# Down projection of a fused attention and feed-forward kernel: tokens as the stationary operand, or weights as the stationary operand with tokens streamed

## The chip, the core and the metric

The kernel runs on one core of one Trainium2 chip. The metric is the device time of one execution in microseconds. TensorE (PE) multiplies and can only write PSUM; VectorE (DVE) and ScalarE (ACT) work on SBUF and PSUM; GpSimd (POOL) does little here; SyncE (SP) issues nearly all DMAs from one queue, in order. A matmul has a stationary operand, loaded into the array by a weight load (PEld in the profile), and a streamed operand whose columns pass through; it may use a part of the array's rows or columns.

## What is computed

x has 2048 tokens of 576 features. The output is x plus two branches of the same layer-normalised x. All is bfloat16.

```python
xn = _layernorm(x, axis=-1)
return x + _A_ref(xn, A_wqkv, A_wo) + _B_ref(xn, B_w_gate, B_w_up, B_w_down)

def _B_ref(x, w_gate, w_up, w_down):          # F = 4608
    g = _silu(x @ w_gate)
    u = x @ w_up
    return (g * u) @ w_down
```

Branch A is attention in 32 heads of 18 features, in which each token looks at itself and at seven earlier ones, two apart (`W, dil = 8, 2`), followed by a product with `wo` (576 x 576).

## The kernel before, in words

Token 16p + r lies in partition p, row r (`R = 16`), so that a 128-token tile is one row of all partitions. The 16 rows are worked in four quarters of 4 rows, 512 tokens (`NTT = 4`, `TT = 512`).

First comes a stage for all tokens: layer norm, transposes into `xnT` (features in partitions), and the q, k, v products (`p_row`, L310). Then for each quarter `tt` of the loop at the end:

- **gate/up**: nine chunks (`NCH`) of four 128-feature tiles. `g_pair` (L611) makes gate and up for two tiles at a time, with the weights `gu` stationary and the quarter's 512 tokens of `xnT` streamed. `g_evac` takes them out of PSUM: ACT applies SiLU (L622) and copies up (L623), DVE multiplies (L624) into `hT`, which holds 36 tiles of 128 features by 512 tokens.
- **down**: for each row `sub`, `d_half` (L640) makes 128 tokens by 576 features: the 128 tokens of `hT` are stationary and 288 columns of `wd` are streamed, over 36 tiles, and then the same over five tiles of the attention output `oT` (which takes the place of `xnT`) with `wo`. The fifth tile of `oT` has its 64 features twice, in the lower and the upper 64 partitions, so that either half of the array's rows can use them.

All large matmuls are halves: one uses 64 rows of the array, its partner the other 64, each into its own bank. With `swap` 0 lower rows make the first bank and upper rows the second; with `swap` 1 they change over, so after both passes every bank holds the sum over all rows. A bank must not be written by both halves at once, so a GpSimd no-op waits for the first pass and the second pass waits for it (`fence_after`, `fence_before`). The second pass leaves the fifth `oT` tile out, since the first has covered both banks with it.

PSUM has eight banks, given out in turn (`new_ps`). A gate/up pair takes four, two rows of the down stage take four. `d_out` adds the residual rows `xr` on DVE (L652) into `ot`, and SP stores one row (L655); in the last row TensorE adds the residual by an identity product and ACT and DVE copy out (L654).

The attention itself is DVE work: `chain(tt)` puts it as a list of closures into `dve` (`Filler`), and `dve.pump(us)` in the loops above emits as much of it as the credit allows, so its place in DVE's queue is fixed when the program is written out: 1.4 us after each `g_evac`, 12.5 and 4.0 us ahead of the two `d_out` of a pair of rows. The chain of quarter tt + 1 is added after chunk 1 of quarter tt. It goes: eight products of `QO` with rows of `Kr` (L418), each with two sums (L423); a mask (L430), maximum, difference, exponential on ACT, sum, reciprocal, product (L438 to L446); eight products with `Vr` (L450) and seven sums (L455), the last of which writes the output over q in `QOP`. `done` doubles the last 64 features into the padding of `QOP`.

At the last chunk of a quarter SP transposes that quarter's four rows of `QOP` into `oT` (L669), loads `xr` in two pieces (L671), and loads the weights of a later chunk: `load_gu(it + 2)` (L182 to L185) comes after each chunk and waits until the chunk's two-deep slot of `gu` is free. In the down stage the stores (L655) stand on SP behind DVE's adds, with a ring load (L398) of the attention between them.

Of the kernel before, what the change touches and what calls it, by code (L numbers as in the profile page):

```python
# [9 lines left out]
bf16 = mybir.dt.bfloat16  # L10
f32 = mybir.dt.float32
ACT = mybir.ActivationFunctionType
ALU = mybir.AluOpType
# [4 lines left out]
P = 128  # L18
H, DH, W, DIL = 32, 18, 8, 2
D = H * DH  # L20
# [4 lines left out]
KT = 5  # L25
DPAD = KT * P
# [4 lines left out]
RT = 4  # L31
NTT = R // RT
TT = RT * P
# [37 lines left out]
def kernel(  # L71
# [11 lines left out]
    nc = tc.nc  # L83
# [3 lines left out]
    NF = F // P  # L87
    NCH = NF // FC

    x_v = A_x.rearrange("b (p r) d -> p (b r) d", r=R)  # L90
    out_v = out.rearrange("b (p r) d -> p (b r) d", r=R)

    const = ctx.enter_context(tc.tile_pool(name="const", bufs=1))
    big = ctx.enter_context(tc.tile_pool(name="big", bufs=1))
# [11 lines left out]
    QOP = big.tile([P, R, DPAD], bf16, name="QO")  # L106
# [3 lines left out]
    hT = big.tile([P, NF, TT], bf16, name="hT")  # L110
    wd = big.tile([P, NF, D], bf16, name="wd")
    wo = big.tile([P, KT, D], bf16, name="wo")
# [2 lines left out]
    mx = big.tile([P, RT, H], f32, name="mx")  # L115
    ssum = big.tile([P, RT, H], f32, name="ssum")
    gu = big.tile([P, NSLOT, 9, FC * P], bf16, name="gu")
    xr = big.tile([P, RT, D], bf16, name="xr")
    kv_d = dram.tile([2, NTT - 1, P, RT * D], bf16, name="kv_d")


# [1 line left out]
    XC, XN = RT * D, RT * DPAD  # L123
# [9 lines left out]
    stage = [hTf[:, o + i * XC:o + (i + 1) * XC].rearrange("p (r d) -> p r d", d=D) for i in range(4)]  # L133
    L = PP[:, 1, 0:2 * W * RT * H].bitcast(f32).rearrange("p (w r h) -> p w r h", w=W, r=RT)
    oT = xnT
    xcT = PP[:, 0, 0:DPAD].rearrange("p (k t) -> p k t", t=P)
    xn0 = A[:].rearrange("p w r h -> p (w r h)")[:, 0:DPAD]

# [40 lines left out]
    def load_gu(it):  # L179
        ch, slot = it % NCH, it % NSLOT  # L180
        fc = slice(ch * FC * P, (ch + 1) * FC * P)
        nc.sync.dma_start(gu[:, slot, 0:4, :], B_w_gate[0:512, fc].rearrange("(kt kp) n -> kp kt n", kp=P))  # L182
        nc.sync.dma_start(gu[:, slot, 4:8, :], B_w_up[0:512, fc].rearrange("(kt kp) n -> kp kt n", kp=P))
        nc.sync.dma_start(gu[0:64, slot, 8, :], B_w_gate[512:576, fc])
        nc.sync.dma_start(gu[64:128, slot, 8, :], B_w_up[512:576, fc])  # L185
# [10 lines left out]
    def new_ps(name):  # L196
        return ps.tile([P, 512], f32, name=name, tag="ps")
# [124 lines left out]
    def fence_after(mm):  # L322
        f = nc.gpsimd.engine_nop()
        tc.add_manual_dep(f.ins, mm.ins.name, SYNC, reason="first half done")
        return f

    def fence_before(mm, f):
        tc.add_manual_dep(mm.ins, f.ins.name, SYNC, reason="banks change row tiles")
# [66 lines left out]
    def ring_load(m, tt):  # L395
        ring = Kr if m == 1 else Vr
        s0 = (HALO + RT * tt) % NRING
        nc.sync.dma_start(ring[:, s0:s0 + RT, :], kv_d[m - 1, tt - 1].rearrange("p (r d) -> p r d", d=D))  # L398


    dve = Filler()
    chains = [0]

    def pieces(tt, w):
        s = (HALO + RT * tt - 2 * w) % NRING
        n = min(RT, NRING - s)
        return [(0, n, s)] + ([(n, RT, 0)] if n < RT else [])

    def chain(tt):
        rows = slice(RT * tt, RT * tt + RT)  # L410
        prod = PP[:, 0, :].rearrange("p (r c) -> p r c", c=D)
        acc = PP[:, 1, :].rearrange("p (r d h) -> p r d h", d=DH, h=H)
        pv = PP[:, 0, :].rearrange("p (r d h) -> p r d h", d=DH, h=H)
        Lr = L.rearrange("p w r h -> p r h w")

        def mul(w):
            for a, b, s in pieces(tt, w):
                nc.vector.tensor_tensor(prod[:, a:b], QO[:, RT * tt + a:RT * tt + b, :],  # L418
                                        Kr[:, s:s + b - a, :], op=ALU.mult)

        def red(w, h):
            rs = slice(2 * h, 2 * h + 2)
            nc.vector.tensor_reduce(L[:, w, rs], prod[:, rs].rearrange("p r (h d) -> p r h d", d=DH),  # L423
                                    axis=AX.X, op=ALU.add)

        def mask():
            for w in range(1, W):
                n = min(RT, max(0, 2 * w - RT * tt))
                if n:
                    nc.vector.memset(L[0:1, w, 0:n, :], NEG)  # L430

        bc = lambda t: t[:].unsqueeze(1).to_broadcast([P, W, RT, H])
        for w in [0] + list(range(W - 1, 0, -1)):
            dve.add(1.3, lambda w=w: mul(w))
            for h in range(2):
                dve.add(1.2, lambda w=w, h=h: red(w, h))
        dve.add(0.4, mask)
        dve.add(1.2, lambda: nc.vector.tensor_reduce(mx[:], Lr, axis=AX.X, op=ALU.max))  # L438
        dve.add(1.2, lambda: nc.vector.tensor_tensor(L, L, bc(mx), op=ALU.subtract))  # L439
        if tt + 1 < NTT:  # L440
            dve.add(0.0, lambda: ring_load(1, tt + 1))
        dve.add(2.0, None)
        dve.add(1.0, lambda: nc.scalar.activation(L, L, ACT.Exp, scale=SCALE))  # L443
        dve.add(1.2, lambda: nc.vector.tensor_reduce(ssum[:], Lr, axis=AX.X, op=ALU.add))
        dve.add(0.3, lambda: nc.vector.reciprocal(ssum[:], ssum[:]))
        dve.add(1.2, lambda: nc.vector.tensor_tensor(A[:], L, bc(ssum), op=ALU.mult))  # L446

        def pvm(w, dst):
            for a, b, s in pieces(tt, w):
                nc.vector.tensor_tensor(dst[:, a:b], Vr[:, s:s + b - a, :].rearrange("p r (d h) -> p r d h", h=H),  # L450
                                        A[:, w, a:b].unsqueeze(2).to_broadcast([P, b - a, DH, H]), op=ALU.mult)

        def pva(w):
            dst = acc if w else QO[:, rows, :].rearrange("p r (d h) -> p r d h", h=H)
            nc.vector.tensor_tensor(dst, acc, pv, op=ALU.add)  # L455

        for w in range(W - 1, -1, -1):
            dve.add(1.4, lambda w=w: pvm(w, acc if w == W - 1 else pv))
            if w < W - 1:
                dve.add(1.3, lambda w=w: pva(w))  # L460
        if tt + 1 < NTT:
            dve.add(0.0, lambda: ring_load(2, tt + 1))

        def done():
            nc.vector.tensor_copy(QOP[:, rows, D:DPAD], QOP[:, rows, 512:D])
            chains[0] += 1
        dve.add(0.3, done)
# [15 lines left out]
    def turn(r):  # L483
        return lambda: transp_halves(r)
# [20 lines left out]
    t = [new_ps("qkv_ps") for g in range(NG)]  # L505
# [39 lines left out]
    t = p_row(2, turn(3))  # L545
# [6 lines left out]
    t = p_row(3, turn(4))  # L552
# [10 lines left out]
    for r in range(4, R):  # L563
        t = p_row(r)
# [53 lines left out]
    def g_evac(ch, j):  # L618
        t = ring_ps[j]
        sg = tmp.tile([P, TT], bf16, name="sg", tag="sg", bufs=3)  # L620
        uc = tmp.tile([P, TT], bf16, name="uc", tag="uc", bufs=3)
        nc.scalar.activation(sg[:], t[0][:], ACT.Silu)  # L622
        nc.scalar.copy(uc[:], t[1][:])  # L623
        nc.vector.tensor_tensor(hT[:, ch * FC + j, :], sg[:], uc[:], op=ALU.mult)  # L624
# [22 lines left out]
    def d_out(r, sub, t):  # L647
# [6 lines left out]
            (nc.scalar.copy, nc.vector.tensor_copy)[h](ot[:, cols], t[h][:, 0:HALF])  # L654
        nc.sync.dma_start(out_v[:, r, :], ot[:])  # L655

    for tt in range(NTT):
        for ch in range(NCH):
            it = tt * NCH + ch
            for p in range(2):  # L660
                g_pair(tt, ch, p)
                for j in (2 * p, 2 * p + 1):
                    g_evac(ch, j)
                    if it % NCH < NCH - 1 or p == 0:
                        dve.pump(1.4)
            if ch == NCH - 1:
                dve.drain(lambda: chains[0] > tt)
                for r in range(RT * tt, RT * tt + RT):
                    nc.sync.dma_start_transpose(oT[:, :, r * P:(r + 1) * P], QOP[:, r, :])  # L669
                for i in (0, 2):  # L670
                    nc.sync.dma_start(xr[:, i:i + 2, :], x_v[:, RT * tt + i:RT * tt + i + 2, :])  # L671
            if it + NSLOT < NTT * NCH:
                load_gu(it + NSLOT)
            if tt == 0:
                if 1 <= ch <= 7:
                    load_wd(ch - 1)
                if ch in (3, 4):
                    load_wd(11 - ch)
                for _ in range(3 if ch in (1, 2) else 2):
                    if wo_order:  # L680
                        load_wo(wo_order.pop(0))
                if ch == 0:
                    store(2, 3, 3)
            if ch == 1 and tt < NTT - 1:
                chain(tt + 1)
        for sub in range(0, RT, 2):
            t, fence = {}, {}
            for swap in range(2):
                for i in (sub, sub + 1):
                    d_half(tt, i, swap, t, fence)  # L690
                    if swap:
                        dve.pump(12.5 if i == sub else 4.0)
                        d_out(RT * tt + i, i, t[i])
# [30 lines left out]
```

## Time and profile before

| | |
|---|---|
| median of 3 runs | 503.17 us (502.95 to 503.41) |
| the profiled execution | 503.37 us, span 501.6 us, granted TensorE clock 1.0 |
| gate/up stages | 59.56, 169.18, 278.80, 388.42 us from the span's start, 69.93 us each |
| down stages | 129.49, 239.11, 348.73 and 458.35 us, the first three 39.69 us each |
| matmul of 512 columns on 64 rows (L611) | 376 ns each, 2592 of them |
| matmul of 288 columns on 64 rows (L640) | 283 ns each, 2596 of them |
| weight load, 64 rows x 128 columns | 94 ns each |
| add of the residual (L652), 128x288 | 451 ns each, 30 of them |
| transpose by DMA of one row (L669) | 2.6 us from issue to landing |

A duration of a matmul is its whole passage; matmuls overlap, so their cost is the distance between starts. A stretch of the table by stretch counts the instructions that lie in it in part, so neighbours add a few. The chain that ended last is followed back from the end, and its shares say which engine set the time.

### The profile page before, as it was taken

The numbers are of one execution on the slowest core, as the hardware profiler recorded it, in microseconds if no ns is written. First come the engines' busy times: TensorE is split into PE (matmuls) and PEld (weight loads), VectorE is DVE, ScalarE is ACT, GpSimd is POOL, SyncE is SP. The second block draws the span as 40 slices with busy tenths as digits, with TensorE's granted clock in tenths as the row PEclk, the third lists the DMA queues.
The fourth block names the chain that finished last, engine by engine and source line by source line (L and its number), as shares of the span: only waits on it lengthen the run. The fifth ranks groups of instructions, "written<-read, shape, count | busy, mean of one in ns | idle before, by whom it ended". The sixth has DMA issues, their size and how long they took to land.

```text
span 501.6 us, 13271 instructions
## 1 busy us (share of the span) xinstructions
PE 497.6 (99%) x5795; PEld 283.1 (56%) x5795; DVE 329.3 (66%) x479; ACT 200.9 (40%) x416; POOL 2.7 (1%) x9
## 2 busy tenths in 40 slices
PE   9999999999999999999999999999999999999997
PEld 4555544444677644444777544445777444446775
DVE  5888597898999698999897139995980222221001
ACT  4756657645300255554300445557000454553000
POOL 1000000000000000000000000000000000000000
PEclk9999999999999999999999999999999999999999
DMA  8799989898731045535640154453700335432200
GB/s 311 175 205 238 306 271 293 259 322 260 194 117 61 25 143 189 190 110 177 158 132 29 31 182 153 132 189 110 183 25 14 101 115 177 158 127 39 76 14 25
DMA packets 77186, 75.42 MB, mean 150 GB/s; under 512 B 22708, under 2 KB 72528, under 8 KB 77128
## 3 DMA queue, kind: packets, MB, share of 16 engines
q1 hardware_dynamic: 76840, 73.98, 49.7%
q8 instruction: 45, 0.74, 0.6%
q10 hardware_dynamic: 288, 0.59, 0.3%
q14 instruction: 13, 0.11, 0.1%
HBM read 58.76 MB, written 5.90 MB: 129 GB/s over the span
## 4 chain that ended last, share of the span: by engine, by line
PE 99%; DVE 0%; issue 0%
PE g_ps L611 56%; PE d_ps L640 32%; PE qkv_ps L310 11%; PE warm_ps L174 1%; PE pt L271 0%; DVE ot L654 0%; PE pt L292 0%; PE warm_ps L271 0%; PE warm_ps L177 0%
## 5 line engine op out<-in xcount | busy, mean ns | idle before, releaser
L611 PE MATMUL g_ps<-xnT,gu 64*128 64x512 bf16 x2592 | 280.4, 376 | 0.0
L611 PEld LDWEIGHTS <-gu 64*128 64x128 bf16 x2592 | 126.1, 94 | 152.9
L622 ACT ACTIVATE sg<-g_ps 128x512 bf16<-128x512 f32 x144 | 87.3, 606 | 156.6 <-PE g_ps L611 156.6
L640 PE MATMUL d_ps<-wd,hT 64*128 64x288 bf16 x2304 | 146.3, 283 | 0.0
L640 PEld LDWEIGHTS <-hT 64*128 64x128 bf16 x2304 | 112.0, 94 | 29.8
L624 DVE TENSOR_TENSOR hT<-sg,uc 128x512 bf16<-128x512 bf16 x144 | 60.2, 419 | 93.9 <-ACT uc L623 93.8
L623 ACT CAST uc<-g_ps 128x512 bf16<-128x512 f32 x144 | 85.2, 592 | 0.0
L423 DVE TENSOR_REDUCE PP<-PP 128x64 f32<-128x1152 bf16 x64 | 84.9, 1347 | 0.4
L310 PE MATMUL qkv_ps<-hT,xnT 64*128 64x432 bf16 (+1 forms) x536 | 50.0, 342 | 0.0
L418 DVE TENSOR_TENSOR PP<-QO,Kr 128x2304 bf16<-128x2304 bf16 (+1 forms) x35 | 43.5, 1251 | 7.3 <-DMA Kr<-hT 6.9
L652 DVE TENSOR_TENSOR ot<-d_ps,xr 128x288 bf16<-128x288 f32 x30 | 12.3, 451 | 51.0 <-PE d_ps L640 51.0
L450 DVE TENSOR_TENSOR PP<-Vr,A 128x2304 bf16<-128x2304 bf16 (+1 forms) x35 | 43.3, 1251 | 0.4
L310 PEld LDWEIGHTS <-xnT 64*128 64x128 bf16 (+1 forms) x536 | 26.1, 94 | 22.3 <-ACT xnT L296 0.2
L455 DVE TENSOR_TENSOR PP<-PP 128x2304 bf16<-128x2304 bf16 x24 | 32.5, 1354 | 0.3
L622 ACT ACT_TABLE_LOAD x5 | 6.4, 1283 | 47.2 <-PE g_ps L611 47.2
L640 PE MATMUL d_ps<-wo,xnT 64*128 64x288 bf16 x288 | 22.9, 283 | 0.0
L372 ACT CAST hT<-qkv_ps 128x288 bf16<-128x288 f32 (+2 forms) x58 | 20.9, 423 | 0.0
L443 ACT ACTIVATE PP<-PP 128x1024 f32<-128x1024 f32 x4 | 4.2, 1056 | 31.3 <-DVE PP L439 31.2
L640 PEld LDWEIGHTS <-xnT 64*128 64x128 bf16 x288 | 14.0, 94 | 3.6
L654 ACT CAST ot<-d_ps 128x288 bf16<-128x288 f32 x1 | 0.4, 399 | 38.8 <-PE d_ps L640 38.8
L372 ACT CAST QO<-qkv_ps 128x432 bf16<-128x432 f32 (+1 forms) x30 | 12.2, 406 | 8.3 <-PE qkv_ps L310 8.2
L221 DVE BATCH_NORM_STATS2 stats<-wd 128x6 f32<-128x288 bf16 x32 | 12.8, 440 | 0.0
(56 smaller groups left out, 92.1 us busy)
## 6 DMA issues: line engine op xcount, KB each, us to landing
gu<-in_B_w_gate_dram SPq DMA_DIRECT2D x36, 512.0 KB, 3.8
gu<-in_B_w_up_dram SPq DMA_DIRECT2D x36, 512.0 KB, 5.2
wd<-in_B_w_down_dram SPq DMA_DIRECT2D x9, 576.0 KB, 6.2
kv_d<-hT SPq DMA_DIRECT2D x5, 576.0 KB, 6.1
gu<-in_B_w_gate_dram SPq DMA_DIRECT2D x36, 64.0 KB, 4.9
gu<-in_B_w_up_dram SPq DMA_DIRECT2D x36, 64.0 KB, 4.5
xr<-in_A_x_dram SPq DMA_DIRECT2D x8, 288.0 KB, 3.9
out_dram<-ot SPq DMA_DIRECT2D x16, 144.0 KB, 1.8
```

What stands on the lines that cost most here:

```text
L221: nc.vector.bn_stats(sums[r][:, k, :], xc[:, j, k * HALF:(k + 1) * HALF])
L310: return nc.tensor.matmul(t[g][:, 0:G], xT_of(r)[rows, kt, :], w_at(g, kt, rows), start=start, stop=stop)
L372: (nc.vector.tensor_copy if n in dve else nc.scalar.copy)(*parts[n])
L418: nc.vector.tensor_tensor(prod[:, a:b], QO[:, RT * tt + a:RT * tt + b, :], Kr[:, s:s + b - a, :], op=ALU.mult)
L423: nc.vector.tensor_reduce(L[:, w, rs], prod[:, rs].rearrange("p r (h d) -> p r h d", d=DH), axis=AX.X, op=ALU.add)
L450: nc.vector.tensor_tensor(dst[:, a:b], Vr[:, s:s + b - a, :].rearrange("p r (d h) -> p r d h", h=H), A[:, w, a:b].unsqueeze(2).to_broadcas ...
L455: nc.vector.tensor_tensor(dst, acc, pv, op=ALU.add)
L611: mm = nc.tensor.matmul(ring_ps[j][b][:], gu[rows, slot, k, fc], xnT[rows, kt, tok], start=(swap == 0 and kt == 0), stop=(swap == 1 and kt ...
L622: nc.scalar.activation(sg[:], t[0][:], ACT.Silu)
L623: nc.scalar.copy(uc[:], t[1][:])
L624: nc.vector.tensor_tensor(hT[:, ch * FC + j, :], sg[:], uc[:], op=ALU.mult)
L640: mm = nc.tensor.matmul(t[sub][h][:, 0:HALF], a[rows], w[rows, h * HALF:(h + 1) * HALF], start=(swap == 0 and n == 0), stop=(swap == 1 and ...
```

## The change

In quarters 0, 1 and 2 the down stage is turned round. `dT_pair` has 128 features of `wd` (and `wo`) stationary and streams the quarter's 512 tokens of `hT` (and `oT`): two feature tiles at a time, with row halves and `swap` as before, so four tiles make 512 features. `dT_rest` makes the last 64 features: all 128 rows of the array, 64 of its columns for the first 256 tokens and the other 64 columns for the last 256, into one bank, 41 tiles one after the other; the 41st has 64 rows.

The sums now have features in partitions. So the residual is needed that way too: `load_xT` loads x over the quarter's rows of `QOP` once these have been transposed into `oT`, and transposes it by DMA into `xT`. `dT_out` adds on DVE in `xT` and transposes back by DMA into `QOP`, from where `dT_store` stores three pieces; the last 64 features of rows 2 and 3 lie in the padding of rows 0 and 1. `xr` is now a view of `xT`, used in the last quarter alone, whose down stage is as before.

```diff
+    def load_xT(tt):
+        r = RT * tt
+        nc.sync.dma_start(QOP[:, r:r + RT, 0:D], x_v[:, r:r + RT, :])
+        nc.sync.dma_start(QOP[:, r:r + 2, D:DPAD], x_v[:, r + 2:r + 4, 512:D])
+        for i in range(RT):
+            n = KT if i < 2 else KT - 1
+            nc.sync.dma_start_transpose(xT[:, 0:n, i * P:(i + 1) * P], QOP[:, r + i, 0:n * P])
+
+    def dT_pair(tt, q, swap, t, fence):
+        tok = slice(tt * TT, (tt + 1) * TT)
+        tiles = [(hT[:, f, :], wd[:, f, :]) for f in range(NF)]
+        tiles += [(oT[:, k, tok], wo[:, k, :]) for k in range(KT - swap)]
+        if not swap:
+            t[q] = [new_ps("d_ps") for h in range(2)]
+        for n, (a, w) in enumerate(tiles):
+            for half in range(2):
+                rows = slice(64 * half, 64 * half + 64)
+                h = half ^ swap
+                m = 2 * q + h
+                mm = nc.tensor.matmul(t[q][h][:], w[rows, m * P:(m + 1) * P], a[rows],
+                                      start=(swap == 0 and n == 0), stop=(swap == 1 and n == len(tiles) - 1))
...
+    def dT_rest(tt):
+        lo = tt * TT
+        t = new_ps("d_ps")
+        tiles = [(hT[:, f, :], wd[:, f, 512:D], 0) for f in range(NF)]
+        tiles += [(oT[:, k, :], wo[:, k, 512:D], lo) for k in range(KT)]
+        for n, (a, w, lo) in enumerate(tiles):
+            rows = slice(0, P if n < len(tiles) - 1 else 64)
+            for b in range(2):
+                nc.tensor.matmul(t[64 * b:64 * b + 64, 0:2 * P], w[rows],
+                                 a[rows, lo + 2 * P * b:lo + 2 * P * (b + 1)],
+                                 start=n == 0, stop=n == len(tiles) - 1)
+        return t
+
+    def dT_out(tt, m, t):
+        n = TT if m < KT - 1 else 2 * P
+        r = RT * tt
+        nc.vector.tensor_tensor(xT[:, m, 0:n], t[:, 0:n], xT[:, m, 0:n], op=ALU.add)
+        nc.sync.dma_start_transpose(QOP[:, r:r + n // P, m * P:(m + 1) * P], xT[:, m, 0:n])
+
+    def dT_store(tt):
+        r = RT * tt
+        nc.sync.dma_start(out_v[:, r:r + 2, :], QOP[:, r:r + 2, 0:D])
+        nc.sync.dma_start(out_v[:, r + 2:r + 4, 0:512], QOP[:, r + 2:r + 4, 0:512])
+        nc.sync.dma_start(out_v[:, r + 2:r + 4, 512:D], QOP[:, r:r + 2, D:DPAD])
...
-                for i in (0, 2):
-                    nc.sync.dma_start(xr[:, i:i + 2, :], x_v[:, RT * tt + i:RT * tt + i + 2, :])
+                if tt < NTT - 1:
+                    load_xT(tt)
+                else:
+                    for i in (0, 2):
+                        nc.sync.dma_start(xr[:, i:i + 2, :], x_v[:, RT * tt + i:RT * tt + i + 2, :])
...
+        if tt < NTT - 1:
+            t, fence = {}, {}
+            for swap in range(2):
+                for q in range(2):
+                    dT_pair(tt, q, swap, t, fence)
+                    if swap:
+                        dve.pump(12.5 if q else 21.0)
+                        for h in range(2):
+                            dT_out(tt, 2 * q + h, t[q][h])
+            t = dT_rest(tt)
+            dve.pump(3.0)
+            dT_out(tt, KT - 1, t)
+            dT_store(tt)
+            continue
```

More of the change, by code (lines that the diff above doesn't have):

```diff
@@ L117 @@
     gu = big.tile([P, NSLOT, 9, FC * P], bf16, name="gu")
-    xr = big.tile([P, RT, D], bf16, name="xr")
+    xT = big.tile([P, KT, TT], bf16, name="xT")
     kv_d = dram.tile([2, NTT - 1, P, RT * D], bf16, name="kv_d")
@@ L135 @@
     oT = xnT
+    xr = xT[:].rearrange("p k t -> p (k t)")[:, 0:XC].rearrange("p (r d) -> p r d", d=D)
     xcT = PP[:, 0, 0:DPAD].rearrange("p (k t) -> p k t", t=P)
@@ L655, in d_out @@
         nc.sync.dma_start(out_v[:, r, :], ot[:])
+    def load_xT(tt):
[18 more added lines that the diff above has]
+                                      start=(swap == 0 and n == 0), stop=(swap == 1 and n == len(tiles) - 1))
+                if not swap and n == len(tiles) - 1 and half == 1:
+                    fence[q] = fence_after(mm)
+                if swap and n == 0 and half == 0:
+                    fence_before(mm, fence[q])
```

## The prediction

> **What bounds the kernel now.** I read the busy shares first, then the chain that ended last, then the table by stretch, cut where the first matmul of each stage starts in the timeline.
>
> ```profile
> span 501.6 us, 13271 instructions
> PE 497.6 (99%) x5795; PEld 283.1 (56%) x5795; DVE 329.3 (66%) x479; ACT 200.9 (40%) x416; POOL 2.7 (1%) x9
> ...
> PE g_ps L611 56%; PE d_ps L640 32%; PE qkv_ps L310 11%; PE warm_ps L174 1%; PE pt L271 0%; DVE ot L654 0%; PE pt L292 0%; PE warm_ps L271 0%; PE warm_ps L177 0%
> ```
>
> The chain is TensorE from end to end: whatever PE gains or loses moves the end, and what other engines gain is worth nothing until PE waits for it. The table by stretch prices the stages (first column the stretch, then the sum, then PE, weight loads, DVE, ACT, POOL, clock, DMA share, GB/s):
>
> ```profile
> 59.56:129.49 69.93, 69.93 (x651) 31.54 (x649) 63.68 (x82) 41.88 (x80) 0.00 (x0) 1.00 0.91 283
> 129.49:169.18 39.69, 39.69 (x651) 31.43 (x649) 37.37 (x40) 3.73 (x5) 0.00 (x0) 1.00 0.33 90
> ...
> 239.11:278.80 39.69, 39.69 (x651) 31.59 (x649) 32.35 (x34) 3.73 (x5) 0.00 (x0) 1.00 0.39 104
> ...
> 348.73:388.42 39.69, 39.69 (x651) 31.59 (x649) 26.29 (x29) 1.39 (x3) 0.00 (x0) 1.00 0.30 74
> ```
>
> A gate/up stage is 648 matmuls of 512 columns, a down stage 648 of 288 (the few more are neighbours cut by the window). Both run as pairs, one matmul on each half of the array's rows. So a pair takes 69.93/324 = 0.2158 us at 512 columns and 39.69/324 = 0.1225 us at 288: 0.0933 us for 224 columns, 0.4165 ns a column, with 2.5 ns fixed. PE has no gap at a granted clock of 1.00. DVE is busy 37.37 of 39.69 us in the first of these stages: that one has almost no room.
>
> **The arithmetic of PE, per turned stage.** Removed: 39.69 us. Added: two feature pairs, each 41 + 40 pairs of 512 columns, 162 x 0.2158 = 34.97 us. Then the last 64 features: 41 steps of two matmuls of 256 columns, one for each column half of the array. No matmul of the trace of before stands in a column half. If the two run beside each other as the two row halves do, a step costs 0.1225 - 32 x 0.0004165 = 0.1092 us, 4.48 us in all; if they run one after the other, 8.95 us; if each also waits for its own weight load (98 ns in the 128x128 rows), 82 x 0.207 = 17.0 us. I take 4.48: the nearest rows are the row halves, which do run together, and the column halves write other partitions of their bank. Sum 39.45, **-0.24 us a stage, -0.7 us in three**. That is all there is to gain: the products are the same, each matmul still has its own weight load (there are 726 fewer of each among 5796), and loads were hidden already (PEld is busy 31 of 39.69 us). Only the fixed 2.5 ns of 121 fewer steps goes.
>
> On this choice the Trainium skill (TensorE: Matmul & The Clock Gate, Part 3) speaks for it: three column tiles of 32 reached 2.38 times. No row of before shows it; by it the step stays at 0.109 us.
>
> **Changes of array shape.** The kernel of before has one from 128-row to 64-row matmuls, at 10.2 us:
>
> ```profile
> 9.37 1.36 PE L310 MATMUL qkv_ps<-hT,PP 128*128 128x432 bf16 x8
> 10.57 1.80 PE L310 MATMUL qkv_ps<-hT,xnT 64*128 64x432 bf16 x18
> ...
> 10.20 0.11 PEld L310 LDWEIGHTS <-PP 64*128 64x128 bf16 x4 [0.36 <-issue]
> ```
>
> From 9.37 to 10.57 stand four whole matmuls and two pairs, six steps of 0.1825 us (2.5 ns + 432 columns) = 1.10 us; it took 1.20. The weight loads paused 0.36 us: the load of the new shape isn't brought ahead. So a change costs 0.10 us. A turned stage has three (64x128 to 128x64; the 41st tile, 64 rows, to 64x64; back to 64x128): **+0.3 us a stage, +0.9 in three**. Bounds: 0, and 0.38 each (0.283 us of a matmul's own duration plus a load of 0.094), 3.4 us.
>
> **PSUM and DVE at the end of the stage.** Four pair banks and one for the rest are taken in turn from eight, so the second gate/up pair of the next quarter (PE start + 3.89 us) takes pair banks and, for its second chunk, 5 steps or 1.08 us later, the bank of the rest. The adds that free them stand in DVE's queue behind attention work: in the first turned stage five mask products with their sums come before the first two adds, the softmax and two products before the next two, a sum and a product before the last. Durations from the rows of before: five groups of 4.03 us from 131.26, then 1.42 + 1.31: 154.2. The first feature pair is done at 129.49 + 122 x 0.2158 = 155.8, so DVE waits; two adds at 0.65 us each (128x288 takes 0.41 in the timeline; 224 columns more at 1.07 ns, the slope between L374's DVE rows of 144 and 432 columns, 360 and 669 ns) to 157.2. The sum, mask, maximum, difference, exponential, sum, reciprocal, product and two PV products take 13.1 us as they do in before, to 170.3; two adds to 171.6; 1.36 + 1.36 us; the last add ends at 174.8. With the concurrent rest PE enters gate/up at 129.49 + 39.45 + 0.3 = 169.24 and asks for that bank at 169.24 + 3.89 + 1.08 = 174.2: **PE stalls 0.7 us, once**. Bounds: 0 if DVE is 0.7 us quicker, 1.1 us if the four long adds take 0.75 us, L374's 432-column row stretched to 512. In the second and third stage attention is done before the last adds (DVE has 32.35 and 26.29 us of work), no stall. Behind the waiting adds on DVE stand the gate/up products; ACT has three buffers before it waits for those, so nothing comes sooner.
>
> **SyncE.** Its queue is in order.
>
> ```profile
> 129.69 5.21 SPq L669 DMA_TRANSPOSE xnT<-QO  x4
> 134.94 1.05 SPq L671 DMA_DIRECT2D xr<-in_A_x_dram  x2
> 136.04 2.10 SPq L182 DMA_DIRECT2D gu<-in_B_w_gate_dram  x1
> ...
> 177.15 0.39 SPq L182 DMA_DIRECT2D gu<-in_B_w_gate_dram  x1
> ```
>
> Four transposes of five blocks cost SP 1.30 us each and land in 2.6. The residual now waits for them (it overwrites their source), about 136.2, lands 6.9 us later (the row of the other 576 KB loads of x), then four transposes: SP free at 148.3, xT there at 150.9. Covers: first add at 155.8, 5 us (without them the add and its banks slip); the weights of the next quarter's chunk 1, issued behind this at 148.3, are needed at 177. At nothing, then. At the end of the stage: last add 174.8, its transpose and landing 2.6, three stores at about 0.5: SP reaches the load of chunk 2 at 179 (first stage). Its slot is free at 169.24 + 7.77 + 0.7 = 177.7. Before, it was issued from 177.15 to 179.3 with landings of 3.8 to 5.4 us, for use at 184.7: about 1 us to spare. Late by 1.3, beside 0.59 MB of stores: **0.3 us**, bounds 0 and 2. In the other two stages the add follows the rest at once, SP is free 2 us before the slot.
>
> DVE's own work falls a little (8 adds of 0.41 go, 4 of 0.65 and one of 0.38 come), hidden. The last quarter is unchanged.
>
> **Sum.** -0.7 + 0.9 + 0.7 + 0.3 = +1.2 us on the profiled execution's 503.37 (span 501.6, 1.8 around it): 504.6. The median of the runs, 503.17, lies 0.2 lower: **504.4 us**. Only 0.2%, about 1 us, can be told from no change.
>
> **Rivals.**
> 1. The column halves run in turn: 34.97 + 8.95 + 0.3 - 39.69 = +4.53 a stage. The stall and the late load vanish (PE comes later than DVE). 503.17 + 13.6 = 516.8. For it: no row shows column halves together, both stream through the same rows, and they share a bank. Against it: their weights and PSUM partitions are apart. 0.22.
> 2. They run together, but a step waits for one weight load: 41 x 0.207 = 8.5, +4.1 a stage, 515.4. For it: two loads must fit into 0.109 us; against: at 7.82 us two whole matmuls of 128 columns start 0.055 us apart, each with a 128x128 load. 0.10. The Trainium skill (TensorEngine Tiling, Restrictions) has column tiling without fast weight load; at the 64/1.2 = 53 ns a load of its TensorE page, an estimate, two fit just, and one that shows makes it 510.
> 3. No load is brought ahead and nothing runs together: 17.0, +12.6 a stage, 541. Against it the same rows: whole-array loads overlap matmuls on the same rows. 0.04. This is what the Trainium skill's rule (TensorE page, Part 3, What overlaps), overlap only across different row groups, would give; the trace disagrees for the whole array.
> 4. Not slower: DVE is ahead of the bank of the rest and changes of shape hide behind running matmuls; decided by whether the last add of the first stage ends before 174.2 and whether loads pause. 503.17 - 0.7 = 502.5. 0.13.
> 5. Transposes and stores on SP are twice as slow, so the load of chunk 2 is late in all three stages by about 2 us: 510. 0.06.
>
> The forecast has 0.45: 503.4 to 506, some 0.13 of it within 0.2%. Faster by over 0.2% needs more than the 0.7 us there is plus luck: 0.03. Within 0.2%: 0.10 of rival 4 and 0.13: 0.23. Slower: 0.74. Forecast and rivals 2 and 5 hold 0.61, so the range must take in rival 1: 502.9 to 517.5; the forecast's own is 503.4 to 506.
>
> **What would show it.** PE between the first turned matmul and the next gate/up one: 39.7 us right, 44.2 rival 1, 52 rival 3. Starts of the 64x256 matmuls: 0.109 us for two, or each. Idle PE near 174 released by DVE: the bank; idle PE near 184 released by a DMA: the load; pauses of weight loads at each change of shape. It would be wrong if 512-column pairs with weights from the down matrix took other than 0.2158 us.

## The result, and the profile after

The changed kernel takes 504.28 us (median of 13 runs, 503.67 to 504.96); before took 503.12 us in the 13 runs beside them (502.94 to 503.41). The ratio is 1.0022, 95% interval 1.0013 to 1.0030: slower by 1.2 us. The forecast was 504.4 us. The profiled execution of the changed kernel took 503.92 us, one of the shorter ones.

The head of the page after, and its chain:

```profile
span 502.1 us, 11840 instructions
PE 498.0 (99%) x5069; PEld 306.1 (61%) x5069; DVE 329.1 (66%) x470; ACT 201.0 (40%) x416; POOL 2.7 (1%) x9
...
PE 98%; DMA 1%; DVE 0%; SPq 0%; issue 0%
PE g_ps L612 56%; PE d_ps L681 21%; PE qkv_ps L311 11%; PE d_ps L641 8%; PE d_ps L698 3%; DMA hT<-in_A_wqkv_dram 1%; PE pt L293 0%; DVE ot L655 0%; SPq L146 0%; PE pt L272 0%; PE warm_ps L272 0%
```

TensorE still is the chain, and its 726 matmuls and weight loads fewer bought nothing. The DMA in the chain lies in the first 6 us, in code that the change doesn't touch; the start of the first gate/up stage moves by up to 0.9 us from execution to execution (59.22 us here, 59.56 in before, 60.09 in another profile of this same kernel). So traces are compared below from the start of the first gate/up stage to the start of the last down stage: 59.56 to 458.35 = 398.79 us in before, 59.22 to 458.89 = 399.67 us here, **+0.88 us**.

The table by stretch of the changed kernel, cut at the first matmul of each stage (columns as before):

```profile
129.15:168.98 39.83, 39.83 (x409) 30.39 (x404) 35.62 (x36) 3.79 (x5) 0.00 (x0) 1.00 0.39 100
168.98:239.08 70.10, 70.10 (x651) 36.47 (x651) 65.28 (x83) 36.67 (x70) 0.00 (x0) 1.00 0.53 166
239.08:279.04 39.96, 39.96 (x409) 22.82 (x405) 28.47 (x27) 3.92 (x6) 0.00 (x0) 1.00 0.43 106
279.04:348.98 69.94, 69.94 (x650) 31.28 (x650) 47.61 (x63) 40.44 (x74) 0.00 (x0) 1.00 0.45 146
348.98:388.95 39.97, 39.95 (x408) 21.84 (x405) 26.77 (x27) 1.40 (x3) 0.00 (x0) 1.00 0.43 91
```

The down stages went from 39.69 to 39.83, 39.96 and 39.97 us, and the gate/up stage behind the first of them from 69.93 to 70.10. A busy share can't show why, since PE counts as busy while it waits behind a matmul in flight. The chain in order of time can (start, length, what). It counts a stage from the end of the piece before it, the table from the stage's first matmul, up to 0.35 us earlier (239.43 against 239.08), so single stages differ between the two while their sums agree to 0.06 us:

```profile
129.38 34.97 PE d_ps L681 x324
164.34 4.71 PE d_ps L698 x82
169.05 70.38 PE g_ps L612 x648
239.43 34.97 PE d_ps L681 x324
274.40 4.71 PE d_ps L698 x82
279.11 70.04 PE g_ps L612 x648
349.15 7.77 PE d_ps L681 x72
356.92 0.02 issue
356.94 27.37 PE d_ps L681 x252
384.31 4.71 PE d_ps L698 x82
389.02 70.04 PE g_ps L612 x648
```

The feature pairs take 34.97 us, to the hundredth what 162 pairs of 0.2158 us make. Then each of the three groups of stages carries the same 34.97 + 4.71 + 70.04 = 109.72 us against 39.69 + 69.93 = 109.62 before, **+0.10 us**. Two of them carry a wait in addition: 70.38 in place of 70.04, **+0.34 us**, after the first turned stage, and 7.77 + 0.02 + 27.37 in place of 34.97, **+0.19 us**, in the third. 0.30 (three times 0.10) + 0.34 + 0.19 is 0.83 of the 0.88 us.

**The column halves and the changes of shape.** The timeline about the last 64 features, PE and weight loads:

```profile
164.27 3.85 PEld L698 LDWEIGHTS <-wd 128*64 128x64 bf16 x72 [0.42 <-issue]
164.27 4.12 PE L698 MATMUL d_ps<-hT,wd 128*64 128x256 bf16 x72
168.12 0.44 PEld L698 LDWEIGHTS <-wo 128*64 128x64 bf16 x8
168.22 0.83 PE L698 MATMUL d_ps<-xnT,wo 128*64 128x256 bf16 x10
168.76 0.10 PEld L698 LDWEIGHTS <-wo 64*64 64x64 bf16 x2 [0.20 <-issue]
168.98 0.33 PEld L612 LDWEIGHTS <-gu 64*128 64x128 bf16 x6
168.99 0.60 PE L612 MATMUL g_ps<-xnT,gu 64*128 64x512 bf16 x4
```

72 matmuls start from 164.27 on and the next at 168.22: 36 steps of two in 3.95 us, 0.110 us a step. So the halves run together. Weight loads pause where the shape changes (0.42 and 0.20 us without one), and at each change the next matmul starts late: the 41 steps and their end cost 4.71 in place of 41 x 0.1092 = 4.48 us, and the gate/up stage 70.04 in place of 69.93.

**The bank.** The last add of the first turned stage, and TensorE's weight loads beside it:

```profile
172.56 1.36 DVE L451 TENSOR_TENSOR PP<-Vr,A 128x2304 bf16<-128x2304 bf16 x1
...
173.84 0.42 DVE L706 TENSOR_TENSOR xT<-d_ps,xT 128x256 bf16<-128x256 f32 x1
...
174.31 0.76 PEld L612 LDWEIGHTS <-gu 64*128 64x128 bf16 x9 [0.47 <-issue]
```

The add ends at 174.26, behind a PV product of the attention (a product with `Vr`); the loads and with them the matmuls that need its bank go on at 174.31. They were due at 168.99 + 3.89 + 1.08 = 173.96.

**A wait that the forecast didn't have.** The start of the third turned stage:

```profile
348.99 7.93 PE L681 MATMUL d_ps<-hT,wd 64*128 64x512 bf16 x72
349.18 6.23 SPq L727 DMA_TRANSPOSE xnT<-QO  x4
356.88 0.38 SPq L662 DMA_DIRECT2D QO<-in_A_x_dram  x1
356.90 0.79 PEld L681 LDWEIGHTS <-wo 64*128 64x128 bf16 x10 [0.48 <-issue]
356.94 1.25 PE L681 MATMUL d_ps<-xnT,wo 64*128 64x512 bf16 x10
```

The first attention tile streams all 512 tokens, so it needs all four transposes of the attention output; before, the first row's matmuls needed only the first of them. They usually take SP 5.2 us and were landed 0.8 us ahead of the need in the first stage. Here one of the four took SP 2.32 us (the median is 1.27), all took 6.23, and the tile, due 7.77 us after the stage began, came 0.18 us late.

This is not chance alone. In all ten profiles of turned kernels the four transposes of the third stage take SP 5.69 to 6.32 us, against 5.20 to 5.23 in the first two stages, and 5.18 in the third stage of before. What lies beside the slow one is a transfer on a queue that the profile lists as `instruction`; the page of the changed kernel has

```profile
q8 instruction: 39, 0.64, 0.6%
```

One of these 39 runs from 352.96 to 354.34 us, and the slow transpose from 353.09 us on. In before the one nearest in time starts at 354.19 us, behind the transposes, and there a load of `xr` takes SP 1.30 us. From 100 us on, the eleven profiles of this document have 58 long issues on SP (over 0.9 us, transposes over 1.5 us). All 58 overlap a transfer on an instruction queue (q8 or q14), and so do only 208 of the 2130 others. No experiment moved these transfers alone, so that they cause the long issues is likely and not shown.

### The profile page after: what moved, and what is told of

Same layout as the page of the kernel before. It is cut to its first block, busy times and chain, and to the rows that moved or that the text cites. A ratio compares the mean times of both kernels' runs of the same rounds, so it can differ in the third digit from the quotient of the medians.

```text
span 502.1 us, 11840 instructions
## 1 busy us (share of the span) xinstructions
PE 498.0 (99%) x5069; PEld 306.1 (61%) x5069; DVE 329.1 (66%) x470; ACT 201.0 (40%) x416; POOL 2.7 (1%) x9
## 2 busy tenths in 40 slices
DMA packets 94124, 78.96 MB, mean 157 GB/s; under 512 B 38884, under 2 KB 90240, under 8 KB 94072
## 4 chain that ended last, share of the span: by engine, by line
PE 98%; DMA 1%; DVE 0%; SPq 0%; issue 0%
PE g_ps L612 56%; PE d_ps L681 21%; PE qkv_ps L311 11%; PE d_ps L641 8%; PE d_ps L698 3%; DMA hT<-in_A_wqkv_dram 1%; PE pt L293 0%; DVE ot L655 0%; SPq L146 0%; PE pt L272 0%; PE warm_ps L272 0%
## 5 line engine op out<-in xcount | busy, mean ns | idle before, releaser
L612 PEld LDWEIGHTS <-gu 64*128 64x128 bf16 x2592 | 151.4, 94 | 128.0 <-issue 0.5
L681 PE MATMUL d_ps<-hT,wd 64*128 64x512 bf16 x864 | 96.3, 376 | 0.0
L681 PEld LDWEIGHTS <-wd 64*128 64x128 bf16 x864 | 55.6, 94 | 38.0
L311 PEld LDWEIGHTS <-xnT 64*128 64x128 bf16 (+1 forms) x536 | 42.8, 94 | 5.8 <-ACT xnT L297 0.2
L641 PE MATMUL d_ps<-wd,hT 64*128 64x288 bf16 x576 | 36.6, 283 | 0.0
L641 PEld LDWEIGHTS <-hT 64*128 64x128 bf16 x576 | 28.1, 94 | 7.4
L706 DVE TENSOR_TENSOR xT<-d_ps,xT 128x512 bf16<-128x512 f32 (+1 forms) x15 | 9.0, 632 | 23.2 <-PE d_ps L681 16.3
L653 DVE TENSOR_TENSOR ot<-d_ps,xT 128x288 bf16<-128x288 f32 x6 | 2.5, 453 | 31.6 <-PE d_ps L641 31.6
```

Of the source, the lines that this page charges most:

```text
L311: return nc.tensor.matmul(t[g][:, 0:G], xT_of(r)[rows, kt, :], w_at(g, kt, rows), start=start, stop=stop)
L612: mm = nc.tensor.matmul(ring_ps[j][b][:], gu[rows, slot, k, fc], xnT[rows, kt, tok], start=(swap == 0 and kt == 0), stop=(swap == 1 and kt ...
L641: mm = nc.tensor.matmul(t[sub][h][:, 0:HALF], a[rows], w[rows, h * HALF:(h + 1) * HALF], start=(swap == 0 and n == 0), stop=(swap == 1 and ...
L681: mm = nc.tensor.matmul(t[q][h][:], w[rows, m * P:(m + 1) * P], a[rows], start=(swap == 0 and n == 0), stop=(swap == 1 and n == len(tiles) ...
```

## Experiments

My theory (A): the time over before is the changes of shape (some 0.3 us in all) and waits of TensorE for things that come just in time, so that they differ from run to run: the bank of the last 64 features, the first attention tile, the load of chunk 2. The rival (B): these waits are incidental, and the rest of the cost is spread, by more DMA traffic (94124 packets against 77186) or ahead of the first gate/up stage. "Inner stretch" is again the start of the first gate/up stage to that of the last down stage in each profile.

| kernel | median, us (runs) | before beside it | difference | inner stretch against before's 398.79 |
|---|---|---|---|---|
| changed, again | 504.32 (11) | 503.12 | +1.20 | +0.64 |
| add first | 503.57 (11) | 503.12 | +0.45 | +0.44 |
| attention tiles later | 503.89 (11) | 503.12 | +0.77 | +0.69 |
| both | 503.58 (11) | 503.12 | +0.46 | +0.29 |
| both, again | 503.81 (11) | 503.16 | +0.65 | +0.35 |
| both, one change of shape fewer | 503.49 (11) | 503.16 | +0.33 | -0.06 |
| the same, again | 503.34 (11) | 503.13 | +0.21 | -0.07 |
| and the stores later | 503.27 (11) | 503.13 | +0.14 | -0.07 |
| halves in turn | 517.66 (2) | 503.16 | +14.50 | +14.45 |

**The changed kernel again.**

> The changed kernel as it is, as the measure for the three beside it. Theory A (the cost is three changes of array shape per turned stage, 0.33 us against 0.24 us saved, plus waits of TensorE for the first attention tile and for the bank of the last 64 features, which differ from run to run) and theory B (the rest of the cost is not in these two waits but spread over more DMA traffic or lies ahead of the first gate/up stage) both expect 504.0 to 504.6 us, +0.9 to +1.4 over before.

504.32 us, ratio 1.0020 (1.0011 to 1.0029). In this profile the wait for the bank is there (70.36 us), the wait for the attention tile is not (34.97 in all three stages). The four transposes of the third stage are slow here too, 5.77 us, but not slow enough to be waited for. So the place of the second wait recurs, and its size is a matter of the run.

**The last add first.**

```diff
             t = dT_rest(tt)
-            dve.pump(3.0)
             dT_out(tt, KT - 1, t)
+            dve.pump(3.0)
             dT_store(tt)
```

> The last add of a turned stage goes ahead of the 3 us of attention that stood before it on VectorE. Theory A: the bank of the last 64 features is free some 2.5 us sooner, the gap of 0.13 us near 174 us is gone and the load of chunk 2 comes sooner: 0.1 to 0.4 us less than the changed kernel. Theory B: no difference, within 0.1 us.

503.57 us, ratio 1.0008 (0.9999 to 1.0017), 0.75 us less than the changed kernel, more than theory A asked for; its slowest run (504.10) is faster than the changed kernel's median. So B doesn't hold as the whole account: one add moved by 3 us on an engine that isn't the bound did this. A longer stretch ahead of the first gate/up stage, the second half of B, isn't tested by it. In its profile the gap near 174 is gone, and another of the waits shows instead:

```profile
169.62 70.18 PE g_ps L612 x648
...
279.48 70.04 PE g_ps L612 x648
```

The second and the last of the four loads of chunk 2 in its timeline:

```profile
178.40 1.22 SPq L184 DMA_DIRECT2D gu<-in_B_w_up_dram  x1
...
180.22 0.60 SPq L186 DMA_DIRECT2D gu<-in_B_w_up_dram  x1
```

The extra 0.14 us begins at 185.3, where chunk 2's matmuls begin: of its four loads, issued from 177.73 on, the second took SP 1.22 us in place of 0.51 (an instruction transfer runs from 178.34 to 179.22 us), and the last, issued at 180.22, took 5.2 us to land (185.4). In the changed kernel's own profile that last load was issued later, at 180.57, but landed in 4.2 us, in time. So this load too comes just in time.

**The attention tiles later.** In the first pass, both feature pairs' feed-forward tiles, then both pairs' attention tiles:

```diff
-            for swap in range(2):
-                for q in range(2):
-                    dT_pair(tt, q, swap, t, fence)
+            for part in "ho":
+                for q in range(2):
+                    dT_pair(tt, q, 0, t, fence, part)
+            for q in range(2):
+                dT_pair(tt, q, 1, t, fence)
...
```

> In the first pass the attention tiles of both feature pairs come after the 36 feed-forward tiles of both, so the first attention tile is needed 15.5 us after the stage begins instead of 7.8. Theory A: no gap of TensorE at the first attention tile whatever one transpose takes on SyncE; 0.2 to 0.7 us less than the changed kernel, and a spread of runs nearer to the 0.5 us of before than to its 1.3 us. Theory B: no difference within 0.1 us and the same spread.

503.89 us, ratio 1.0014 (1.0005 to 1.0023), 0.43 us less than the changed kernel, with a spread of 0.98 us against its 1.26. The direction is as A expected; the intervals overlap, so the size isn't settled, and the spread, which A expected nearer to 0.5 us, came out nearer to the old one. Its profile has the bank's wait (70.39) and, as it must, none for attention tiles.

**Both.** The two edits together.

> Both of the above. Theory A: only the changes of array shape are left, +0.3 us over before for the three stages: 503.3 to 503.7 us. Theory B: 504.0 to 504.6 us like the changed kernel.

503.58 us, ratio 1.0006 (0.9997 to 1.0014), spread 0.63 us. A second time, beside the next kernel:

> Both moves again, as the measure beside the next kernel: 503.3 to 503.8 us, +0.3 to +0.6 over before; each turned stage and the gate/up stage behind it 0.10 us longer than in before (three changes of array shape at 0.33 us together against 0.24 us saved).

503.81 us, ratio 1.0011 (1.0002 to 1.0019), just above what was expected (503.8, and +0.65 where +0.6 was the limit). The same kernel thus reads 503.58 and 503.81: medians 0.2 us apart don't tell two kernels from one another. The gains don't add: with the add moved, the later tiles brought nothing more that the medians show (503.57 against 503.58 and 503.81). The chain of this kernel (the first of the two) is the clean case:

```profile
129.62 34.97 PE d_ps L682 x324
164.58 4.71 PE d_ps L699 x82
169.30 70.04 PE g_ps L612 x648
239.33 34.97 PE d_ps L682 x324
274.30 4.71 PE d_ps L699 x82
279.01 70.04 PE g_ps L612 x648
```

No wait is left, each group of stages is 109.72 us, and the inner stretch is 0.29 us over before: what the changes of shape cost beyond what the pairs save.

**One change of shape fewer.** The 41st tile keeps 128 rows; its weights, which are there twice in `wo`, are copied once into a tile whose other 64 rows are zero.

```diff
+    woz = const.tile([P, 64], bf16, name="woz")
+    nc.gpsimd.memset(woz[:], 0.0)
+                if ch == NCH - 1:
+                    nc.gpsimd.tensor_copy(woz[0:64], wo[0:64, KT - 1, 512:D])
...
-        tiles += [(oT[:, k, :], wo[:, k, 512:D], lo) for k in range(KT)]
+        tiles += [(oT[:, k, :], wo[:, k, 512:D] if k < KT - 1 else woz[:], lo) for k in range(KT)]
...
-            rows = slice(0, P if n < len(tiles) - 1 else 64)
```

> Both moves, and the 41st tile of the last 64 features keeps 128 rows: its stationary operand has the 64 weights in the lower rows and zeros in the upper ones, so a turned stage has two changes of array shape instead of three. If a change costs 0.10 us because the weights of the new shape aren't loaded ahead: 0.3 us less than both moves alone, within 0.2 us of before, and no step of 0.20 us at the 41st tile. If what is left is not the changes of shape: same as both moves alone.

503.49 us, ratio 1.0006 (0.9997 to 1.0015), 0.32 us less than both moves beside it (503.81), as expected, but 0.33 over before where at most 0.2 was expected. Its timeline:

```profile
168.63 0.60 PE L700 MATMUL d_ps<-xnT,wo 128*64 128x256 bf16 x8
168.96 0.11 PEld L700 LDWEIGHTS <-woz 128*64 128x64 bf16 x2
169.07 0.28 PE L700 MATMUL d_ps<-xnT,woz 128*64 128x256 bf16 x2
169.27 0.76 PEld L614 LDWEIGHTS <-gu 64*128 64x128 bf16 x10 [0.20 <-issue]
```

The 41st tile starts 0.11 us after the 40th, and only one pause of weight loads is left here. In each of the three stages the 82 matmuls take 4.60 in place of 4.71 us in the chain, and the inner stretch is 398.73 us, 0.06 under before. A second time, beside the next kernel:

> The kernel with both moves and two changes of shape again, as the measure beside the next: 503.3 to 503.6 us, +0.1 to +0.4 over before.

503.34 us, ratio 1.0004 (0.9996 to 1.0013).

**The stores later.**

```diff
                 load_gu(it + NSLOT)
+            if tt and ch == 0:
+                dT_store(tt - 1)
...
-            dT_store(tt)
```

> In addition the three stores of a turned stage go behind the load of the next quarter's chunk 2 on SyncE, so that this load no longer waits until the sums are turned back. If what is left over before in the median (some 0.3 us, though the traced execution has none of it between the first gate/up stage and the last down stage) is TensorE's wait for that load in some runs: 0.1 to 0.3 us less than the kernel beside it, within 0.1 us of before, and a spread of about 0.5 us. If it is something else: no difference within 0.1 us.

503.27 us, ratio 1.0003 (0.9994 to 1.0012), 0.07 less than the kernel beside it, with a spread of 0.91 us (0.73 beside it). Within the noise that is the second reading: no gain, so what is left is not shown to be the load of chunk 2. No version beats before.

**The halves in turn.**

```diff
-        for n, (a, w, lo) in enumerate(tiles):
-            rows = slice(0, P if n < len(tiles) - 1 else 64)
-            for b in range(2):
+        for b in range(2):
+            for n, (a, w, lo) in enumerate(tiles):
+                rows = slice(0, P if n < len(tiles) - 1 else 64)
```

> The changed kernel with the last 64 features made in turn: all 41 steps of one column half, then all 41 of the other. If the two column halves run together only when their matmuls alternate, a turned stage grows by 41 x 0.109 = 4.5 us less what this hides of the wait for the bank: +12.5 to +13.5 us over the changed kernel, 517 to 518. If the halves did not gain from each other, no change.

517.66 us, ratio 1.0286 (1.0267 to 1.0305), 13.3 us over the changed kernel.

```profile
129.54 34.97 PE d_ps L681 x324
164.51 9.41 PE d_ps L698 x82
173.92 70.04 PE g_ps L612 x648
```

9.41 in place of 4.71 us for the same 82 matmuls: they run together only when they alternate. The forecast's rival 1 had this at 516.8. The bank's wait is gone, since TensorE comes to it 4.7 us later. In the third stage the four transposes take SP 6.10 us, and the feature pairs 35.03 in place of 34.97 us: the wait for the first attention tile again, 0.06 us.

## Why the prediction was right, point by point

- **What bounds.** Right: TensorE end to end, and nothing on another engine counted until TensorE waited for it.
- **Pairs of 512 columns at 0.2158 us.** Right: 34.97 us.
- **The column halves run together, 0.1092 us a step.** Right: 0.110 us from 72 matmuls; in turn 9.41 us. The Trainium skill (TensorE: Matmul & The Clock Gate, Part 3) measured 2.38 times the speed for three column tiles of 32. The trace agrees that column tiles run together: 4.71 us for the two halves alternating, 9.41 in turn. The rule of the Trainium skill in the same part (What overlaps and what doesn't), that a weight load overlaps a matmul in flight only in another row group, doesn't hold here: two loads of 110 ns each, on the same 128 rows, stand within each step of 0.110 us.
- **Changes of shape, 0.10 us each, 0.3 a stage.** Right: 109.72 - (34.97 + 4.48 + 69.93) = 0.34 us for three, and 0.11 us back when one was taken out.
- **The bank, 0.7 us once.** Right in mechanism, mis-sized: 0.34 us. Most of the difference is arithmetic: the prediction's own terms give 155.82 + 1.30 + 13.1 + 1.30 + 2.72 + 0.38 = 174.62, not 174.8, against 174.21, a wait of 0.4 us. With the stage 0.34 us earlier the add would end at 174.28; it ended at 174.26. Two small errors cancelled there: the first add began 0.27 us later than forecast, and instructions in a row on DVE overlap a little (the next starts up to 0.1 us before the one ahead ends). TensorE in turn came 0.1 us later than forecast.
- **The load of chunk 2, 0.3 us.** Right that it is late: issued from 178.95 us on, 1.8 us later than before, and TensorE comes to it just in time. Wrong in size: in the two profiles of the changed kernel it cost nothing, in that of the moved add 0.14 us. The margin of about 1 us was put too low: of the four pieces the last two are small (64 KB) and needed one step later, and the last landed in 4.2 us.
- **Only the fixed 2.5 ns of 121 fewer steps goes.** Nearly right: that is 0.30 us a stage, and the 0.24 of the sum comes from 128 more columns streamed (the 41st step of the last 64 features), 0.05 us.
- **Missing:** the first attention tile, which waits for all four transposes, 0.19 us in one of two profiles of this kernel and 0.06 in that of the halves in turn. I named the transposes' order on SP, and that streaming 512 tokens puts four of them ahead of the first use escaped me.
- **The sum.** +1.2 us forecast, +1.16 measured. That it is this near is luck. What the traces show of the sum is +0.30 (shapes less pairs, forecast +0.2) + 0.34 + 0.19 = 0.83 us in one profile and 0.30 + 0.32 in the other: the wait for the bank was put too large, that for the load wasn't there, one was missed, and some 0.3 to 0.6 us of the medians are in no term of the forecast.

What stays open is these 0.3 to 0.6 us: the profiles show +0.64 and +0.88 us in the inner stretch, the medians +1.16 and +1.20, and the moved add gained 0.75 us in the median where a profile shows 0.34 us of wait. The last versions, whose inner stretch is no longer than before's, are still 0.14 to 0.33 us over before in the median, within their intervals. The traces point to one place. In all eleven profiles the time less the inner stretch and less the start of the first gate/up stage is 45.02 to 45.10 us, so what else differs between executions lies ahead of that stage, which starts between 59.15 and 60.09 us. The second profile of the changed kernel is 1.18 us over that of before, 0.64 of it in the inner stretch and 0.53 ahead of it; TensorE there waits until 9.87 us for a load of `wqkv`, in the first profile until 5.79. But before has one profile alone, so whether a turned kernel starts later on average, and why it should, isn't shown. Longer waits in runs without a profile are not excluded either.

## What to carry to other kernels

On a kernel that is TensorE from end to end, count steps times (fixed part + columns): turning the operands round saved 121 steps of 2.5 ns a stage and paid three changes of array shape of 0.11 us, so keep one shape, or pad the odd tile with zeros to stay in it. When more columns are streamed at a time, look at which inputs must now all be there at the first step: the margin goes from the first of four transposes to the last. And work of the evacuation that stands behind other work on its engine is cheap to move: one add put ahead of 3 us of attention gave back 0.75 of the 1.2 us in the median, of which the traces show 0.34 as the wait that it removed. Last, a queue's issue times from one profile hold for the places where they were read: here the long ones moved with the program, from a load with time to spare onto transposes that TensorE waits for.

## What the runs showed of the hardware

- A change of array shape (64x128, 128x64, 64x64) costs TensorE 0.11 us, and weight loads pause there, 0.42 us behind matmuls of 512 columns and 0.20 behind 256: the load of the new shape isn't brought ahead.
- Two column halves that alternate take the time of one; in turn they take twice that (4.71 against 9.41 us for 82 matmuls, changes of shape included). Their weight load of 64 columns takes 110 ns, longer than the 94 ns of 128 columns in a row half, and is hidden.
- A transpose by DMA takes SP 1.27 us and 2.6 us to landing in the median. Among the 16 of the attention output in the changed kernel's profile one took SP 2.32 us, and the one ahead of it 4.2 us to landing; single plain issues on SP took 1.2 to 1.5 us in place of 0.5. A queue whose consumer has less than 1 us to spare turns that into time.
- Long issues on SP lie beside transfers on the instruction queues: 58 of 58 in eleven profiles, and the one on the transposes recurs 3.9 us into the third stage in both profiles of the changed kernel (353.09 and 353.91 us).
